# Holding one unit's row loads back until the second half of the second-layer weights has been asked for

## The chip, the cores and the metric

One core of a Trainium2 chip. The metric is the time of one execution in microseconds on the device, as a median of several runs; smaller is better. Before the change the kernel took 201.92 us (three runs, 201.52 to 202.05).

## The reference

A linear-attention recurrence (RWKV, batch 4, 8 heads, 768 steps, head size 48) followed by a two-layer feed-forward block with SiLU on its 3072 x 384 output:

```python
for t in range(S):
    cur = np.einsum('bhd,bhe->bhde', u[None] * kt, vt)
    y[:, :, t] = np.einsum('bhd,bhde->bhe', rt, state + cur)
    state = w[None, :, :, None] * state + np.einsum('bhd,bhe->bhde', kt, vt)
...
h = x @ w_in                           # 3072 x 384 -> 2048
g = h * (1.0 / (1.0 + np.exp(-h)))
return (g @ w_out).astype(np.float32)  # 2048 -> 384
```

## The kernel before

The steps are cut into 6 chunks of 128; a *unit* is one chunk of one batch, so there are 24. Each needs three row loads (r, k, v; 192 KB each) on the SyncE queue (SP), into one of six buffers per tensor. Unit 8 therefore reuses the buffers of unit 2.

```python
NIN = 6
def load(i, mid=None):
    ...
    sc, b = unit(i)
    for t, src in ((rin, r), (kin, k), (vin, v)):
        ...
        nc.sync.dma_start(out=t[i % NIN][:, :, 0:D], in_=src[b, :, sc * C:sc * C + C, :]...)
```

The second-layer weights are asked for by GpSimd (POOL), which casts them to 16 bits on the way, in two halves of 768 KB as they arrive:

```python
def wout_part(g):
    nc.gpsimd.dma_start(
        out=wout[:, 8 * g:8 * g + 8, :],
        in_=moe_w_out[1024 * g:1024 * g + 1024, :].rearrange("(f p) n -> p f n", p=128))
```

The stretch that matters, cut. The program gives every engine its instructions in this order. `p2(i, nxt=i + 1)` also holds the next unit's transposes on TensorE (PE); `fill` pops feed-forward pieces (`l1` first layer, `l2` second layer) from a list into TensorE's gaps. Short names such as sdec, kc, ku, vu and rku_f are elementwise products on GpSimd, called after the tile that they write.

```python
    wout_part(0)
    sums(1); state(1); bonus_sum(b_); bonus_vu(b_); nat_kc(b_)     # b_ is unit 5
    wout_part(1)
    fill(1); sums(a); state(a)                                     # a is unit 4
    ...
    for i in range(4):
        load(NIN + i)                                              # units 6, 7, 8, 9
    p2(b_, nxt=b_ + 1, late=True)
    ...
    load(NIN + 4); load(NIN + 5)
    ...
    fillers.extend(l1s(1, 0, 2) + l2s(0))     # 16 first-layer pieces, then 16 on the weights above
    sums(b_); state(b_)
    ...
    front(B + 2)                              # unit 6: v cast, ku, rku_f, kc
    ...
    for i in range(B + 2, NU):
        ...
        fill(2)
        if i + 1 < NU:
            front(i + 1)
        if i >= NIN:
            load(i + NIN)
```

## Time and profile before

| | before |
|---|---|
| time | 201.92 us |
| TensorE busy | 192.0 us of a 200.2 us span |
| second-layer weights asked for / landed | 34.38 and 37.86 / 43.9 and 49.2 |
| first used by TensorE | 48.44 and 51.38 |
| unit 8's r asked for / landed / used | 34.39 / 42.7 / 50.83 |
| unit 8's v asked for / landed | 36.38 / 51.1 |

A transfer has three moments that count: when its queue issues it, when its last byte lands, and when the first reader wants it. Landing to first use is its slack. The profile's lines stand in the prediction below.

### The profile page before, as it was taken

The numbers are of one execution on the slowest core, as the hardware profiler recorded it, in microseconds if no ns is written. First come the engines' busy times: TensorE is split into PE (matmuls) and PEld (weight loads), VectorE is DVE, ScalarE is ACT, GpSimd is POOL, SyncE is SP. The second block draws the span as 40 slices with busy tenths as digits, with TensorE's granted clock in tenths as the row PEclk, the third lists the DMA queues.
The fourth block names the chain that finished last, engine by engine and source line by source line (L and its number), as shares of the span: only waits on it lengthen the run. The fifth ranks groups of instructions, "written<-read, shape, count | busy, mean of one in ns | idle before, by whom it ended". The sixth has DMA issues, their size and how long they took to land.

```text
span 200.2 us, 5013 instructions
## 1 busy us (share of the span) xinstructions
PE 192.0 (96%) x1973; PEld 129.8 (65%) x1973; DVE 115.1 (58%) x233; ACT 97.9 (49%) x225; POOL 115.2 (58%) x145
## 2 busy tenths in 40 slices
PE   7789999898999999999999999999999999999993
PEld 2546878786776976765666765666764666644563
DVE  6787658894757647773746864646863635510121
ACT  2655487798133652049662039662039661069300
POOL 3489969989865783768593767481748370100000
DMA  4999998999889954498521748201120001210022
GB/s 86 201 185 165 181 213 178 178 186 194 170 172 226 245 120 97 103 221 175 114 48 40 163 114 161 43 0 43 39 84 0 0 3 41 78 43 0 0 79 79
DMA packets 82207, 22.34 MB, mean 112 GB/s; under 512 B 75400, under 2 KB 82184, under 8 KB 82184
## 3 DMA queue, kind: packets, MB, share of 16 engines
q1 hardware_dynamic: 78504, 18.88, 43.7%
q0 software_dynamic: 3680, 3.15, 10.3%
q8 instruction: 15, 0.25, 0.5%
q14 instruction: 8, 0.07, 0.1%
HBM read 20.45 MB, written 4.72 MB: 126 GB/s over the span
## 4 chain that ended last, share of the span: by engine, by line
PE 84%; DVE 6%; POOL 4%; issue 3%; ACT 1%; DVEq 0%; POOLq 0%
PE ops L366 30%; PE hps L354 28%; PE ae L267 10%; PE xs L242 4%; PE y L293 3%; PE yT L342 2%; DVE am L276 2%; PE y L290 2%; POOL ku L180 1%; PE ops L380 1%; PE sps L309 1%; PE spin L125 1%; DVE pif L156 1%; POOL rku_f L186 1%; DVE y L300 1%
## 5 line engine op out<-in xcount | busy, mean ns | idle before, releaser
L357 ACT ACTIVATE gT<-hps 128x256 f16<-128x256 f32 (+1 forms) x128 | 59.5, 495 | 25.1 <-PE hps L354 23.3
L354 PE MATMUL hps<-xT,win 128*128 128x256 f16 (+1 forms) x384 | 69.9, 326 | 0.2
L366 PE MATMUL ops<-wout,gT 128*128 128x384 f16 x368 | 65.8, 326 | 0.0
L354 PEld LDWEIGHTS <-win 128*128 128x128 f16 x384 | 35.2, 98 | 22.1 <-issue 0.9
L366 PEld LDWEIGHTS <-gT 128*128 128x128 f16 x368 | 34.2, 98 | 20.9
L343 ACT COPY xT<-yT 128x384 f16<-128x384 f16 x24 | 11.5, 478 | 56.4 <-PE yT L342 56.4
L276 DVE TENSOR_TENSOR am<-ae,maskM 128x512 f16<-128x512 f32 x24 | 16.6, 691 | 32.5 <-PE ao L269 32.5
L203 POOL TENSOR_TENSOR vu<-vin,rku 128x384 f32<-128x384 f32 x23 | 19.1, 829 | 21.8 <-DVE rku L197 21.7
L370 DVE COPY osb<-ops 128x384 f32<-128x384 f32 x23 | 12.8, 556 | 32.5 <-PE ops L366 32.3
L267 PE MATMUL ae<-rk 48*128 48x128 f32 x192 | 27.7, 285 | 1.0 <-DVE rk L230 1.0
L267 PEld LDWEIGHTS ae<-rk 48*128 48x128 f32 x192 | 23.1, 187 | 8.3 <-issue 5.8
L269 PE MATMUL ao<-rk 48*128 48x128 f32 x192 | 27.7, 285 | 0.0
L253 DVE TENSOR_TENSOR rk<-xs,pif 112x512 f32<-112x512 f32 x40 | 25.6, 680 | 1.7 <-PE xs L242 1.7
L180 POOL TENSOR_TENSOR ku<-kin,u_bc 128x384 f32<-128x384 f32 x24 | 24.1, 1005 | 2.0 <-DMA kin<-in_k_dram 2.0
L186 POOL TENSOR_TENSOR rku_f<-rin,ku 128x384 f32<-128x384 f32 x24 | 24.1, 1005 | 1.9
L191 POOL TENSOR_TENSOR kc<-kin,lamC 128x384 f16<-128x384 f32 x24 | 24.0, 1002 | 0.0
L269 PEld LDWEIGHTS ao<-rk 48*128 48x128 f32 x192 | 23.1, 187 | 0.0
L323 POOL CAST stb<-st 112x384 f16<-112x384 f32 x12 | 6.0, 502 | 22.8 <-DVE st L318 22.8
L300 DVE TENSOR_TENSOR y<-y,vu 128x384 f16<-128x384 f32 x24 | 13.3, 554 | 8.7 <-PE y L293 6.5
L276 DVE TENSOR_TENSOR am<-ao,maskM 128x512 f16<-128x512 f32 x24 | 16.3, 680 | 0.0
L197 DVE TENSOR_REDUCE rku<-rku_f 128x8 f32<-128x384 f32 x24 | 13.2, 549 | 2.4 <-POOL rku_f L186 2.0
L325 POOL TENSOR_TENSOR sdec<-st,pif 112x384 f32<-112x384 f32 x16 | 13.3, 835 | 1.8 <-ACT gT L357 1.1
(74 smaller groups left out, 188.4 us busy)
## 6 DMA issues: line engine op xcount, KB each, us to landing
rin<-in_r_dram SPq DMA_DIRECT2D x24, 192.0 KB, 4.0
kin<-in_k_dram SPq DMA_DIRECT2D x24, 192.0 KB, 3.8
vin<-in_v_dram SPq DMA_DIRECT2D x24, 192.0 KB, 3.8
out_dram<-osb SPq DMA_DIRECT2D x23, 192.0 KB, 2.0
win<-in_moe_w_in_dram POOLq DMA_DIRECT2D x4, 384.0 KB, 6.0
wout<-in_moe_w_out_dram POOLq DMA_DIRECT2D x2, 768.0 KB, 10.4
out_dram<-osh SPq DMA_DIRECT2D x1, 128.0 KB, 1.7
out_dram<-osh SPq DMA_DIRECT2D x1, 64.0 KB, 1.5
```

Source lines behind the costliest of these rows:

```text
L180: nc.gpsimd.tensor_tensor(out=L["ku"], in0=kin[i % NIN][:, :, 0:D], in1=u_bc, op=ALU.mult)
L186: nc.gpsimd.tensor_tensor(out=L["rku_f"], in0=rin[i % NIN][:, :, 0:D], in1=L["ku"], op=ALU.mult)
L191: nc.gpsimd.tensor_tensor(out=kc[i % NKC][:, :, 0:D], in0=kin[n][:, :, 0:D], in1=lamC, op=ALU.mult)
L203: nc.gpsimd.tensor_tensor(out=L["vu"], in0=vin[i % NIN], in1=L["rku"].unsqueeze(2).broadcast_to([128, H, D]), op=ALU.mult)
L253: nc.vector.tensor_tensor(out=rk[:, :, :, 64 * g:64 * g + 64], in0=xs[g][0:PR], in1=lam(g), op=ALU.mult)
L267: nc.tensor.matmul(ae[:, p, :], L["kT"][0:D, p, :], L["rT"][0:D, p, :], start=True, stop=True)
L269: nc.tensor.matmul(ao[:, p, :], L["kT"][64:PR, p, :], L["rT"][64:PR, p, :], start=True, stop=True)
L276: nc.vector.tensor_tensor(out=am, in0=a, in1=maskM.unsqueeze(1).broadcast_to([128, NP, C]), op=ALU.mult)
L300: nc.vector.tensor_tensor(out=L["y16"], in0=L["y"], in1=L["vu"], op=ALU.add)
L354: nc.tensor.matmul(hps, win[:, q, ft * 128:(ft + 1) * 128], xts[sc][:, q, b0:b1, :].rearrange("p b t -> p (b t)"), start=(q == 0), stop=(q ...
L357: nc.scalar.activation(out=gts[sc][:, ft, b0 * C:b1 * C], in_=hps, func=AF.Silu)
L366: nc.tensor.matmul(ops, gts[sc][:, ft, b * C:(b + 1) * C], wout[:, ft, :], start=(ft == 0), stop=(ft == NFT - 1))
```

## The change

The intent: weights and rows share the same DMA engines between 37 and 49 us. Unit 8 is wanted later than the weights, so its rows should step aside. A one-column memset by GpSimd into unit 8's r buffer, placed after the second weights request in GpSimd's order, makes the r load wait for it (it overwrites the same bytes), and everything behind it on SP.

```diff
     nat_v(b_)
-    for i in range(4):
-        load(NIN + i)
+    load(NIN)
+    load(NIN + 1)
+    nc.gpsimd.memset(rin[2][:, 0, 0:1], 0.0)
+    load(NIN + 2)
+    load(NIN + 3)
     p2(b_, nxt=b_ + 1, late=True)
```

## The prediction

> **What bounds the kernel now.** I read the page first, its engine shares and the chain that ended last.
>
> ```profile
> PE 192.0 (96%) x1973; PEld 129.8 (65%) x1973; DVE 115.1 (58%) x233; ACT 97.9 (49%) x225; POOL 115.2 (58%) x145
> ...
> PE 84%; DVE 6%; POOL 4%; issue 3%; ACT 1%; DVEq 0%; POOLq 0%
> ```
>
> TensorE (PE) is busy 96% of the span and is 84% of the chain. No transfer is in the chain. A change of transfer order pays only if PE stops waiting for something, and costs only if PE starts to. So the next view was the list of who waited for whom, for PE over the whole span; these are all its rows:
>
> ```profile
> PE y L293 <- DVE am L276: 1.4, 5, 0.4
> PE spin L125 <- DVE wrow L82: 1.3, 1, 1.3
> PE ae L267 <- DVE rk L230: 1.0, 1, 1.0
> PE yT L342 <- DVE y L300: 0.7, 2, 0.5
> PE rows L147 <- ACT cols_sb L134: 0.3, 1, 0.3
> ```
>
> None is a transfer: PE waits for neither weights nor rows. The third view is the timeline of the DMA queue (SP) in the stretch touched:
>
> ```profile
> 33.59 0.71 SPq L71 DMA_DIRECT2D vin<-in_v_dram  x1
> 34.39 0.82 SPq L71 DMA_DIRECT2D rin<-in_r_dram  x1
> 35.31 0.97 SPq L71 DMA_DIRECT2D kin<-in_k_dram  x1
> 36.38 2.82 SPq L71 DMA_DIRECT2D vin<-in_v_dram  x1
> 39.29 4.84 SPq L71 DMA_DIRECT2D rin<-in_r_dram  x1
> 44.23 4.29 SPq L71 DMA_DIRECT2D kin<-in_k_dram  x1
> 48.61 2.24 SPq L71 DMA_DIRECT2D vin<-in_v_dram  x1
> 50.94 0.58 SPq L71 DMA_DIRECT2D rin<-in_r_dram  x1
> ```
>
> Counting three loads per unit from the start, the row at 33.59 is the last of unit 7, 34.39 to 36.38 are unit 8's r, k and v, the next three unit 9's, and 50.94 opens unit 10. Long issues mean a queue that is backing up. GpSimd's (POOL) timeline gives the weights and the place of the new instruction:
>
> ```profile
> 34.38 0.94 POOL L417 DMA_DIRECT2D wout<-in_moe_w_out_dram  x1
> ...
> 37.86 0.94 POOL L417 DMA_DIRECT2D wout<-in_moe_w_out_dram  x1
> 38.82 0.85 POOL L325 TENSOR_TENSOR sdec<-st,pif 112x384 f32<-112x384 f32 x1
> 40.74 1.63 POOL L325 TENSOR_TENSOR sdec<-st,pif 112x384 f32<-112x384 f32 x2 [1.07 <-ACT gT L357]
> ```
>
> Who needs the data, from PE's timeline:
>
> ```profile
> 50.83 0.39 PE L242 MATMUL xs<-ident,rin 64*112 64x64 f32 x8
> 51.06 0.39 PE L242 MATMUL xs<-ident,kin 64*112 64x64 f32 x8
> 51.38 2.12 PE L366 MATMUL ops<-wout,gT 128*128 128x384 f16 x12
> ```
>
> These are unit 8's transposes, then the first matmuls on the second half of the weights; the first half is first used at 48.44. From the two tile views (issue plus time to landing): weights land at 34.38 + 9.5 = 43.9 and 37.86 + 11.3 = 49.2; unit 8's r lands at 34.39 + 8.3 = 42.7 and its v at 36.38 + 14.7 = 51.1. Its k has no recorded landing. So the weights are early by 4.5 and 2.2 us, unit 8's r by 8.1 us. Only v is late: ScalarE's cast at 51.09 waited 0.7 us for it, but ScalarE's next work after that cast is at 55.56, with 3.95 us of idle before it, so this wait reaches nobody.
>
> Last, the DMA view of the stretch 38 to 48 us, in which weights and rows share the engines:
>
> ```profile
> q0 software_dynamic: 1888, 1.43, 93.0%
> q1 hardware_dynamic: 2042, 0.39, 33.0%
> ```
>
> The weights get 0.143 MB/us, the rows 0.039. In the stretch 52 to 58, with rows alone, the same view has 1.30 MB in 6 us, 0.217 MB/us.
>
> **What the Trainium skill says.** "DMA: Bandwidth & Descriptors", section "Queues, rings and completion order": each engine goes round its queue rows at packet granularity. The trace agrees: 1888 and 2042 packets, almost one for one, though the weights' packets are about four times as large (757 against 192 bytes). That is why the rows starve. The same page, "Anatomy of one DMA — SWDGE (gpsimd) path": DMA engines don't wait on semaphores, the issuing sequencer does. So a held r load also holds every later load and store on SP; the first trace can't show that yet. "Perfetto Trace Analysis", section "DMA Instruction — HWDGE (DVE, Sync)": the profiled window of an issue covers descriptor generation and not the data; issues of 0.6 to 4.84 us with landings of 3.4 to 14.7 us agree. "SBUF — State Buffer", "Who interferes with whom": DMA has its own ports and doesn't slow compute engines. The trace agrees: the three-operand products on POOL take 1.00 us in the crowded stretch as outside it.
>
> **The change part by part.**
> 1. *Added*: one memset of one column (128x1) on POOL. A like one stands in the kernel already (L460) and took 117 ns. The order of instructions shows it behind the second weights request and behind one sdec, without a wait of its own. That sdec ends at 38.82 + 0.85 = 39.67; POOL is then idle 1.07 us to 40.74, so the 0.12 us fit in the idle time. Cost on the path: 0.
> 2. *Moved*: unit 8's r load goes from 34.39 to about 39.67 + 0.12 = 39.8, 5.4 us later, and pulls k, v and unit 9 behind it. Nothing else changes its order on any engine.
> 3. *What the weights gain* (estimate): their data begins to flow at about 37 (the DMA view of 34.4 to 37 has 0.01 MB on their queue). Rows come back at about 40.5. In those 3.5 us the weights have the engines alone; the first-layer weights alone ran at 0.57 MB in 3 us (21 to 24), and with smaller packets I take 0.18 MB/us instead of 0.143. That is 0.037 x 3.5 = 0.13 MB more, and 0.13 / 0.143 = 0.9 us earlier: the second half lands at about 48.3 instead of 49.2. PE did not wait for it: gain 0.
> 4. *What the rows lose* (estimate): from 40.5 to the end of the weights (data end about 47.6) they get 7.1 x 0.039 = 0.28 MB: r (0.197 MB) is through at 40.5 + 5.0 = 45.5 and lands at about 46 to 47; 0.08 MB of k are in. At the free rate the remaining 0.12 MB take 0.6 us: k lands at about 48.5 to 49.5, v 1 us later at 49.5 to 51. PE needs r at 50.83 and k at 51.06: margins of about 4 and 2 us. v is no later than before, because what it lost in the queue it gets back when the weights end sooner.
> 5. *Behind it*: unit 9 landed at 48.61 + 4.6 = 53.2 and is transposed at 58.57, margin 5 us. The first store is issued at 59.95; its buffers (four) are first used a second time at 76.33.
> Sum: 0.0 us on the path, so 201.9.
>
> **The rivals.**
> A. *Unit 8's k comes too late and PE stalls.* If the lost time isn't made good and k simply shifts by the hold, about 47 (two loads at 0.039 MB/us from 37) becomes 52.4, and PE, which issues in order, stands 1.3 us at the transposes: 203.2, 0.7% slower. For it: the margin is the smallest here, and v shows a straggling tail (landing 51.1, though the average rate had it through near 49). Against: the engines are over 90% busy in the stretch, so time not given to rows goes to weights, which then end sooner. I give it 15%.
> B. *The weights were a hidden limit and the change gains.* For it: the second half lands only 2.2 us before use. Against: no PE row waits for it, and the 0.52 us that PE stands before 47.61 is VectorE's y, which waits for POOL's vu. At most that 0.5 us could move; 201.4. I give it 10%.
> C. *The hold delays POOL's chain* (sdec, ku, rku_f, kc, vu to PE's transposes at 47.61), if the memset waited for old readers. The order shows no such wait; if 0.1 us leaks, 202.0.
> D. *A backlog on SP reaches later units.* In the stretch 48.4 to 52 the DMA share is 0.72 against 1.26 before it, so there is room to catch up; 0.
>
> **Range and chances.** The centre is 201.9. The three runs before lie within 0.53 us of each other, so chip noise alone needs about 0.4 us each side; rival A adds on the upper side: 201.3 to 202.7. A move of 2% is 4 us. Slower by that needs k to land at 55, 8 us after its old place with a hold of 5.4; faster has no wait to take it from. Faster 1%, within 2% 97%, slower 2%.
>
> **What would show it.** Unit 8's r issued at 39.8 +- 0.5 (step 2); the POOL sdec pair still starting near 40.7 (step 1); weights landing near 43 and 48.3 (step 3); unit 8's v landing between 49.5 and 52 and no transfer among PE's waits (step 4); unit 10's r still issued near 51 (step 5); PE's busy time unchanged at 192. The prediction is wrong if PE shows a wait for kin or rin near 51, or if PE's idle time before 47.6 changes.

## The result, and the profile after

The changed kernel took 201.87 us (median of four runs, 201.67 to 202.24), the kernel before 201.77 us in the same rounds (201.52 to 202.05). The ratio is 1.0006, with a 95% interval of 0.9984 to 1.0028: no difference that is clear of the noise. A run is called slow when it is over 1.5% above the fastest of its kernel, otherwise fast. Ratios here and below are the mean time of one kernel's fast runs over that of the other's fast runs of the same rounds, so they are not quite the ratios of the medians quoted.

Page of the changed kernel, TensorE's line of the engine shares:

```profile
PE 193.3 (96%) x1973; PEld 130.9 (65%) x1973; DVE 115.1 (57%) x233; ACT 98.0 (49%) x225; POOL 115.2 (57%) x146
```

The SP queue's timeline of the changed kernel, from the last load of unit 7:

```profile
33.33 0.82 SPq L71 DMA_DIRECT2D vin<-in_v_dram  x1
40.37 0.37 SPq L71 DMA_DIRECT2D rin<-in_r_dram  x1
40.83 0.54 SPq L71 DMA_DIRECT2D kin<-in_k_dram  x1
41.46 4.26 SPq L71 DMA_DIRECT2D vin<-in_v_dram  x1
...
49.51 0.61 SPq L71 DMA_DIRECT2D rin<-in_r_dram  x1
```

The queue stands still from 34.15 to 40.37, then sends unit 8, and has unit 10's r (last row) out at 49.51, before the 50.94 of the kernel before: no backlog is left. GpSimd's timeline shows what it stood still for:

```profile
35.01 0.94 POOL L417 DMA_DIRECT2D wout<-in_moe_w_out_dram  x1
...
38.50 0.94 POOL L417 DMA_DIRECT2D wout<-in_moe_w_out_dram  x1
39.45 0.85 POOL L325 TENSOR_TENSOR sdec<-st,pif 112x384 f32<-112x384 f32 x1
40.23 0.11 POOL L544 MEMSET rin<- 128x1 f32 x1
41.12 1.63 POOL L325 TENSOR_TENSOR sdec<-st,pif 112x384 f32<-112x384 f32 x2 [0.78 <-ACT gT L357]
```

The memset takes 0.11 us out of GpSimd's idle time. This run of the changed kernel is 0.63 us behind the other already at the first weights request, before anything changed, and 0.38 us at the sdec pair; at 26 us TensorE had waited 0.3 us for first-layer weights. Times of the two traces are therefore best compared from the request on. From request to landing the two halves took 7.3 and 8.3 us (they land at 42.3 and 46.8), against 9.5 and 11.3 before. The last line of the tile view of `wout`, before and then after, has the least, the median and the most of the two:

```profile
DMA to landing us min/median/max: 9.5/10.4/11.3
DMA to landing us min/median/max: 7.3/7.8/8.3
```

Unit 8's r lands at 40.37 + 6.8 = 47.2, its v at 41.46 + 8.2 = 49.6.

Who waited for whom, TensorE in the whole changed kernel, all rows:

```profile
PE y L293 <- DVE am L276: 1.3, 5, 0.4
PE spin L125 <- DVE wrow L82: 1.3, 1, 1.3
PE yT L342 <- DVE y L300: 0.7, 2, 0.5
PE hps L354 <- DMA win<-in_moe_w_in_dram: 0.3, 1, 0.3
PE rows L147 <- ACT cols_sb L134: 0.3, 1, 0.3
```

Still neither second-layer weights nor rows. The stretch table settles where the time went; its columns are the stretch in us, its length, then busy time of TensorE, weight loads, VectorE, ScalarE and GpSimd, granted clock, DMA share and GB/s. Before:

```profile
35.00:45.00 10.00, 9.44 (x135) 7.94 (x132) 8.76 (x19) 8.49 (x24) 8.81 (x11) 1.00 1.20 182
45.00:55.00 10.00, 9.48 (x114) 7.04 (x112) 6.09 (x13) 5.12 (x14) 9.40 (x11) 1.00 1.02 182
```

After:

```profile
35.00:45.00 10.00, 9.44 (x134) 7.99 (x134) 8.73 (x19) 8.50 (x24) 9.10 (x13) 1.00 1.17 179
45.00:55.00 10.00, 9.48 (x115) 7.15 (x114) 6.12 (x13) 5.40 (x15) 9.78 (x11) 1.00 1.08 209
```

TensorE's busy time is the same to the hundredth in both stretches. (The page has 193.3 us in all against 192.0; that excess lies before 20 us, 17.58 against 16.30, where nothing was changed.) The transfers moved by microseconds, and the engine that sets the end did not see it. (The chain of waits looks different, 77% TensorE and 12% GpSimd instead of 84% and 4%. Most of that difference lies before 34 us, where the two kernels are the same. I take it that the chain follows now one, now another of two engines that arrive almost together; that is not tested. From 48 us on it is TensorE in both, but for 0.3% of VectorE at the very end. So the busy times are the safer reading.)

### The profile page after: what moved, and what is told of

Its sections match the earlier page's. It is cut to its first block, busy times and chain, and to the rows that moved or that the text cites. A ratio compares the mean times of both kernels' runs of the same rounds, so it can differ in the third digit from the quotient of the medians.

```text
span 200.5 us, 5014 instructions
## 1 busy us (share of the span) xinstructions
PE 193.3 (96%) x1973; PEld 130.9 (65%) x1973; DVE 115.1 (57%) x233; ACT 98.0 (49%) x225; POOL 115.2 (57%) x146
## 4 chain that ended last, share of the span: by engine, by line
PE 77%; POOL 12%; issue 6%; DVE 3%; ACT 1%; POOLq 0%; DVEq 0%
PE ops L366 30%; PE hps L354 25%; PE ae L267 9%; PE xs L242 4%; POOL kc L191 2%; POOL ku L180 2%; PE y L293 2%; POOL rku_f L186 2%; PE yT L342 2%; POOL sdec L325 2%; PE y L290 2%; POOL vu L203 1%; PE ops L380 1%; PE sps L309 1%; DVE am L276 1%
## 5 line engine op out<-in xcount | busy, mean ns | idle before, releaser
L343 ACT COPY xT<-yT 128x384 f16<-128x384 f16 x24 | 11.4, 476 | 57.2 <-PE yT L342 57.2
## 6 DMA issues: line engine op xcount, KB each, us to landing
rin<-in_r_dram SPq DMA_DIRECT2D x24, 192.0 KB, 4.1
kin<-in_k_dram SPq DMA_DIRECT2D x24, 192.0 KB, 3.6
vin<-in_v_dram SPq DMA_DIRECT2D x24, 192.0 KB, 3.6
out_dram<-osb SPq DMA_DIRECT2D x23, 192.0 KB, 2.0
```

## The experiments

My theory: the weights and unit 8's rows both have slack of some microseconds, the change moves slack from one to the other, and the end sees neither. It follows that more hold costs nothing until the rows' slack is used up; that the hold pays as soon as TensorE really waits for the weights; and that the memset itself is free. Rivals: the hold has a gain and a cost that cancel; the memset costs what the hold gains; lateness is made good later whatever happens.

The first four runs share a chip and a median of 202.00 us for the kernel before.

**A longer hold.** The memset and units 8 to 11 moved behind unit 6's kc:

```diff
-    load(NIN + 2); load(NIN + 3)        # and load(NIN + 4); load(NIN + 5) further on
     ...
     front(B + 2)
+    nc.gpsimd.memset(rin[2][:, 0, 0:1], 0.0)
+    load(NIN + 2); load(NIN + 3); load(NIN + 4); load(NIN + 5)
```

> Unit 8's rows (and units 9 to 11 behind them) are held until GpSimd has done unit 6's kc, about 45.5 us instead of 40. Theory 'slack on both sides' (TensorE waits for neither the weights nor the rows; unit 8's k is needed at 51.2): the weights have drained by 46.5, the rows run at the free rate and r, k, v land near 48, 49 and 50 us, so TensorE still waits for no transfer: 201.8, ratio 1.000 +- 0.002. Rival 'the hold has a cost that something else hides in the changed kernel': 6 us more of hold lose time in proportion, 202.5 or more.

Measured: 201.94 us, ratio 0.9995 (0.9984 to 1.0006). Unit 8's r was asked for at 45.83, 11.4 us later than in the kernel before, and landed at 48.9, v at 50.8. TensorE transposed at 51.25 without a wait (the one wait for a row in this trace, 0.7 us for k, is at 6 us). A cost and a gain that cancel would hardly do so at a second length of hold too; that rival falls.

**A hold past the slack.** The same, behind unit 7's kc in the loop:

```diff
             front(i + 1)
+        if i == B + 2:
+            nc.gpsimd.memset(rin[2][:, 0, 0:1], 0.0)
+            load(NIN + 2); load(NIN + 3); load(NIN + 4); load(NIN + 5)
```

> Positive control: rows held until GpSimd has done unit 7's kc, about 50.1 us. Theory 'slack on both sides': the slack is used up; unit 8's r and k land about 2.6 and 3.4 us after the request, near 52.7 and 53.5, so TensorE stands about 2.2 us at unit 8's transposes (needed 51.2) and the run takes 2.0 to 3.0 us more: 203.8 to 204.8. Rival 'a late row is made good later, the end does not depend on it': within 0.5 us of the kernel before.

Measured: 206.03 us, ratio 1.0201 (1.0187 to 1.0215), outside the expected 203.8 to 204.8. TensorE's timeline has the wait where it was expected:

```profile
53.06 0.53 PE L242 MATMUL xs<-ident,rin 64*112 64x64 f32 x8 [1.88 <-DMA rin<-in_r_dram]
54.05 0.43 PE L242 MATMUL xs<-ident,kin 64*112 64x64 f32 x8 [0.47 <-DMA kin<-in_k_dram]
```

That is 2.35 us of standing, close to the 2.2 expected. The rest is in the stretch table, in the column after GpSimd's, TensorE's granted clock:

```profile
55.00:56.00 1.00, 1.00 (x6) 0.53 (x5) 0.88 (x2) 0.51 (x1) 0.92 (x2) 0.62 1.00 197
56.00:57.00 1.00, 1.00 (x5) 0.48 (x4) 0.56 (x1) 0.00 (x0) 1.00 (x2) 0.50 0.98 187
57.00:58.00 1.00, 1.00 (x13) 0.68 (x11) 0.00 (x0) 0.00 (x0) 0.12 (x1) 0.50 1.06 210
58.00:59.00 1.00, 1.00 (x13) 0.78 (x12) 0.57 (x2) 0.00 (x0) 0.00 (x0) 0.67 1.12 215
```

After the stall the clock falls to half. Lost: 0.38 + 0.50 + 0.50 + 0.33 = 1.71 us. With the wait that is 4.06 us, against 206.03 - 202.00 = 4.03 measured by the medians; the profiled run itself took 206.52, so in it some 0.5 us more stay unexplained. So lateness is not made good later, a stall on TensorE costs its own length and here 1.7 us more, and unit 8's rows have an edge. It lies between a request at 45.8 (no wait) and one at 50.2 (2.35 us of wait); the change asks at 40.4.

**Unit 8's rows never loaded** (a wrong result; relative error 0.29):

```diff
-    for i in range(4):
+    for i in (0, 1, 3):
         load(NIN + i)
```

> Wrong result on purpose: unit 8's three loads are left out, its buffers keep unit 2's rows, so the weights meet 0.6 MB less. Upper bound of what taking unit 8's rows out of the weights' way can be worth. Theory 'slack on both sides': 201.8, ratio 1.000 +- 0.002, the weights land sooner (near 47 instead of 49.2) and nobody notices. Rival 'the weights' landing was a hidden limit and the hold gives its gain back elsewhere': 201.3 or less.

Measured: 201.56 us, ratio 0.998 (0.9968 to 0.9992). The expected landing near 47 was a miss: the weights landed at 44.1 and 49.4, as before, because unit 9's rows took unit 8's place at once. So this run isn't the bound that I meant it to be. The 0.2% is at the edge of what was expected, and no stretch explains it: TensorE is busy 9.44 and 9.48 us in the two stretches above here too. What it comes from stays open; it isn't earlier weights.

**The memset alone**, on a scratch column, nothing held:

```diff
+    scratch = cst.tile([128, 1], FP)
...
-    nc.gpsimd.memset(rin[2][:, 0, 0:1], 0.0)
+    nc.gpsimd.memset(scratch, 0.0)
```

> The memset alone: same size and place in GpSimd's order, but on a scratch column, so no load is held. Theory: 0.11 us inside GpSimd's idle time, 201.8, ratio 1.000 +- 0.002; unit 8's r is asked for near 34.4 and the weights land near 49, as in the kernel before. Rival 'the memset costs and the hold gains the same amount': 0.2 us or more slower than before.

Measured: 201.81 us, ratio 0.9995 (0.9982 to 1.0007); r asked for at 33.7, weights landed at 43.7 and 49.1. The memset is free, and the rival that it hides a gain falls.

The next three share another chip, with 201.74 us for the kernel before. They ask when the hold would pay.

**The weights wanted earlier, without and with the hold.** The second-layer pieces are put after 4 of the 16 first-layer pieces instead of after all 16, in the kernel before and in the changed kernel. The same work in another order, and right results:

```diff
-    fillers.extend(l1s(1, 0, 2) + l2s(0))
+    q = l1s(1, 0, 2)
+    fillers.extend(q[:4] + l2s(0) + q[4:])
```

> The kernel before, with the 16 second-layer pieces put after the first 4 of the 16 first-layer pieces in TensorE's filler list, so the second half of the weights is needed near 45.7 us instead of 51.4 and the first half near 42.9. Rows not held: halves land near 43.9 and 49.2. Theory 'the hold moves the weights' landing and nothing else, and pays only where TensorE waits for them': TensorE waits about 1.0 us for the first half and 2.5 us more for the second, 3.5 us in all: 205.3; and if the clock drops after the stall, as it did in the long hold, up to 1.7 us more, 207. Rival 'the weights don't matter even then': 202.

> The changed kernel with the same early use of the weights. Halves land near 42.3 and 46.8. Theory: about 1.1 us of waiting, 2.4 us less than in the run without the hold (49.2 - 46.8): 203.0, ratio to the unheld early-use kernel about 0.988; more apart if only the unheld one loses its clock. Rival 'the hold is worth nothing anywhere': the two early-use kernels take the same time.

Measured: 208.87 us without the hold (ratio 1.0346, 1.0309 to 1.0384), 203.54 us with it (ratio 1.0079, 1.0066 to 1.0092, over four fast runs of five). Both took longer than expected (205.3 to 207, and 203.0), and both are worse than the kernel before, but in the fast runs the hold now takes 2.6% off (1.0346 / 1.0079). Wait rows of TensorE, without the hold:

```profile
PE ops L366 <- DMA wout<-in_moe_w_out_dram: 4.4, 2, 3.8
```

The profiled run of the held one counts as slow (207.47 us, clock 0.983), so it is not in the ratio. Its trace shows the same kind of loss, though: TensorE stands 3.3 us for the second half, and the clock is at half from 46.50 to 53.32. Leaving it out favours the hold; with it the five held runs average 204.2 us against 208.8, which is 2.2% less. The fast runs show that more than the landing is in the difference: all six unheld runs have a mean clock of 0.984 or 0.992, the four fast held ones 0.999 or 1.0. A clock of 0.992 over a span of 205.6 us is 1.6 us, and 0.984 over 208.0 us is 3.3 us. Taken off the unheld runs' 207.33 to 209.96 us, this leaves 205.7 to 206.6, some 2.2 to 3.1 us above 203.54. The 2.4 us expected of the landing lie in there, but that the landing alone makes them is not shown: no fast held run has a trace, and in the two traces there are the second half landed at 48.3 and 47.3, only 1.0 us apart. The weights were wanted at 44.6 in the trace, earlier than the 45.7 that I had put down, which lengthens the wait of both.

**The hold lifted between the two halves**: the memset moved ahead of the second weights request.

```diff
     nat_kc(b_)
+    nc.gpsimd.memset(rin[2][:, 0, 0:1], 0.0)
     wout_part(1)
```

> The memset moved ahead of the second weights request, so unit 8's r is asked for near 38 us, while the first half is flowing and the engines' queues are filling with weights. Tells how soon rows that come second get their turn. Theory 'a newcomer first waits out what the engines have already queued': the first row packets move 3 to 4 us after the request, about 41.5, as in the changed kernel (40.4 to 44). Rival 'round-robin at once': rows at 0.039 MB/us within 1 us of the request. Time in both: 201.8, ratio 1.000 +- 0.002.

Measured: 201.76 us, ratio 0.9997 (0.9983 to 1.0012). By the packet times in the trace, the first row packet of unit 8 moved at 40.5, 2.6 us after the request at 37.85; the changed kernel's rows, asked for at 40.37, first moved at 43.97. The DMA view of the changed kernel from 40.4 to 43.8 us, all its queue rows:

```profile
q0 software_dynamic: 910, 0.69, 131.1%
```

No row packet at all for 3.4 us. With empty queues (the hold past the slack) the first one came 1.0 us after the request. So rows that come second don't get every other packet at once, which is closer to the first theory than to the second, though 2.6 us is less than it said.

The last three share a third chip, 201.92 us for the kernel before.

**The weights wanted a little earlier**: 8 first-layer pieces ahead instead of 4, to see the hold's effect with a short stall.

```diff
-    fillers.extend(q[:4] + l2s(0) + q[4:])
+    fillers.extend(q[:8] + l2s(0) + q[8:])
```

> As the early use without hold, but 8 first-layer pieces ahead of the second-layer pieces instead of 4, so the second half of the weights is needed near 47.8 and the first near 45.5. Halves land near 43.9 and 49.2. Theory: one wait of about 1.4 us (49.2 - 47.8) and no clock loss, because the stall is short: 203.1, ratio 1.006 to 1.008. If the clock drops all the same: 204.8 or more. Rival 'another cost of the new order, not the weights, made the early-use kernels slow': the same time as with the hold.

> The same with the rows held: halves land near 42.4 and 47.0, both before they are needed. Theory: no wait for a transfer, 201.8, ratio 0.999 to 1.001, and 1.4 us less than the unheld one. Rival (other cost of the order): slower than the kernel before by as much as the unheld one.

Measured: 206.97 us without the hold (ratio 1.0209, 1.0168 to 1.0250, five fast runs of six), 202.85 us with it (ratio 1.0064, 1.0034 to 1.0094). TensorE's waits for the weights, without the hold:

```profile
PE ops L366 <- DMA wout<-in_moe_w_out_dram: 2.7, 1, 2.7
```

With the hold:

```profile
PE ops L366 <- DMA wout<-in_moe_w_out_dram: 0.6, 1, 0.6
```

The second half landed at 49.25 and 47.02, 2.2 us apart, and the waits are 2.1 us apart: as far as the wait goes, the hold is worth just what the landing moves. I had put the need at 47.8; it came at 46.6 and 46.5, so both waits are longer than expected and the held one isn't zero. The unheld one again loses its clock, which I had not expected of a short stall; it is at half from 48.46, within the stall, to 55.28:

```profile
48.00:50.00 2.00, 0.71 (x3) 0.37 (x3) 0.36 (x1) 0.00 (x0) 1.92 (x3) 0.61 1.12 219
50.00:52.00 2.00, 2.00 (x10) 1.09 (x9) 0.00 (x0) 0.92 (x3) 0.89 (x2) 0.50 0.50 97
```

Five of the six unheld runs have a mean clock of 0.982 to 0.992; the one at 1.0 took 204.62 us, all held ones (0.999 or 1.0) 202.61 to 204.79. The rival that the new order itself makes these kernels slow falls for the larger part: the same order with the weights landing sooner is 1.4% faster, and the held trace (202.61 us) is 0.7 us above the kernel before, 0.6 of which is its wait.

**The early use with the hold once more**, for a trace.

> The held early-use kernel once more for a trace, because its profiled run was the one of five that lost its clock (0.983, 207.5 us; the other four 203.1 to 203.6 at 0.999 or 1.0). Theory: with the clock kept, 203.1 to 203.6, one wait of about 3 us for the second half of the weights; if the clock is lost again, about 207.

Measured in one look: 207.75 us, clock 0.991. Here the halves landed at 43.8 and 49.0 in spite of the hold, so TensorE waited 4.8 us for them. Of the six traces that hold the rows as the change does or longer (changed kernel, both longer holds, early use twice, half-early use), five have the second half landing at 46.3 to 47.3 us and this one at 49.0. The hold makes an early landing likely and doesn't guarantee it. The hold worked here too: no row packet moved from 37.56 to 43.34. But the weights were behind before the rows came back: from 38 to 42 us, alone on the engines, they moved 0.67 MB, against 0.78 MB in the changed kernel. Why they were slower stays open.

No version beat the kernel before.

## Why the prediction was right

- *What bounds the kernel* held: TensorE's busy time in the stretch is equal to the hundredth, and no transfer of this stretch is among its waits in either trace.
- *Step 1, the memset* held: 0.11 us (0.12 predicted) inside idle time; alone on a scratch column it cost nothing.
- *Step 2, the move* held in kind: 40.37 against 39.8, just outside the +-0.5 given. The memset ran right after the sdec, and the 0.6 us are the head start that this run lacked before the change.
- *Step 3, what the weights gain* had the right sign, and the term was under-sized: the second half was predicted 0.9 us sooner and came 2.4 us sooner (49.2 to 46.8), 3.0 us counted from the request. Rows were taken to share from 40.5 on; in the trace none moved before 43.97, so the weights had the engines alone for about 7 us (36.7 to 44.0) instead of 3.5, and at 0.69 MB in 3.4 us = 0.20 MB/us instead of 0.18. PE's gain stayed 0, as said.
- *Step 4, what the rows lose* held in its result: r at 47.2 (46 to 47 predicted), v at 49.6 (49.5 to 51), margin on r 4.0 us (about 4). The way there was another, a later start and then a faster finish; that the two errors nearly cancel is luck. k has no recorded landing in either trace; TensorE took it at 51.44 without a wait.
- *Step 5* held: unit 10's r at 49.5, sooner than the 51 predicted and than the 50.94 before.
- *Rival A* (a stall on unit 8) did not happen, and the hold past the slack shows that it was real further out. Its size would have been too small: it counted only the wait, and the run shows 1.7 us of slow clock on top of 2.35. *Rival B* (weights as a hidden limit) fell here, and the early-use runs show the regime in which it would have been right. *Rivals C and D* left no trace.

## What to carry to other kernels

Before reordering transfers, compare landing with first use for both sides: a transfer that lands before its reader asks has no time to give, however busy the DMA engines are. If both sides have slack, the reorder is worth nothing on the clock, but it moves slack, and that can be used up by another change: here the hold was worth 1.4 to 2.6% (fast runs) once the weights were wanted 5 to 7 us sooner. Count a stall on TensorE dearer than its length, since the clock can fall to half with it: here stalls of 2.35 and 2.7 us did that, one of 0.6 us did not.

## What the Trainium skill lacked or had wrong

- "DMA: Bandwidth & Descriptors", section "Queues, rings and completion order", has the engines go round the queue rows at packet granularity. That holds once both are flowing (1888 and 2042 packets in 10 us). It lacks what a newcomer sees: row packets first moved 3.6 us after the request in the changed kernel and 2.6 us in the run with the hold lifted between the halves, while weights were flowing, against 1.0 us with empty queues. The runs don't show where they waited.
- "TensorE: Matmul & The Clock Gate", section "HAM oscillation — how this bites in real kernels", puts the rule at idle gaps over about 3.4 us (its next section, "A second HAM failure mode: psum-queue depth-cycling", has frequent short idles cost the clock too, without a length). Here gaps of 1.88 and 0.47 us close together cost the clock in all four runs of that kernel (mean 0.989 to 0.992), and a kernel whose trace has one gap of 2.7 us lost it in five of six. The depth (0.50) agrees with the page's section "What's actually happening", and so does the length: 1.71 us lost at half clock is 3.4 us; in the half-early run it was 6.8 us, twice that.
